# Input transfers first, the first weight conversion spread over the filter's units, and the fourth pair's last steps moved into the second MLP step

## The chip, the cores and the metric

The kernel runs on one core of one Trainium2 chip. TensorE (PE) multiplies; VectorE (DVE), ScalarE (ACT) and GpSimd (POOL) do the elementwise work; SyncE (SP) issues transfers between HBM and SBUF, which 16 DMA engines carry. The metric is the device time of one execution in microseconds (us); the time before is 1118.43 us, the median of three runs (1118.03 to 1119.11).

## The reference

Three stages follow one another on 6016 tokens of 256 channels. The first is a circular convolution along the sequence, written with Fourier transforms; the other two are MLPs with 2048 hidden units.

```python
X = np.fft.rfft(x, axis=1)                     # x: 2 x 3008 x 256
F = (filt_r + 1j * filt_i)[None, :, :]
x = np.fft.irfft(X * F, n=3008, axis=1).reshape(6016, 256)
h = x @ w_in;  x = np.maximum(0.01 * h, h) @ w_out        # first MLP
h = x @ w_in2; r = np.maximum(h, 0); out = (r * r) @ w_out2   # second MLP
```

The weights come as 64-bit floats and are used as 32-bit floats.

## The kernel before

**The filter.** The length 3008 is split as 47 x 64. The 256 channels are cut into 16 groups of 16, so with two batches there are 32 *units*; unit s is batch s mod 2 of group s // 2. The loop over s (lines 704 to 751) is a software pipeline: iteration s holds the first transform of unit s (`stage_a`, matmul `pa`), its transpose on VectorE (`stage_r`, tile `bin`), the second transform of unit s-1 (`stage_b`, matmul `px`), the product with the filter (`stage_s`: ScalarE copies px to `xc`, VectorE makes `t1` from px and `fr`; `stage_2`: GpSimd makes `t2` from xc and `fi`), the inverse transform of unit s-3 (`stage_i`, matmuls into `zps`) and its transpose (`stage_t`, tile `zin`). `fi` must first get its signs: the first groups by `sign_f` on VectorE or GpSimd, the later ones by `sign_k` on ScalarE, one column a time. Units in `SWAP` need one `zps` matmul instead of two, but an addition before it (`stage_y`, on VectorE for `SWAP_V`, else on GpSimd).

**The last transform** (`stage_o`, matmuls `pi`, and `stage_w`, a copy to SBUF) runs for the first 128 channels inside the loop's second half, and for the other 128 after it (`fill`), 16 groups of 4 matmuls each; four PSUM tiles take turns, so a group needs the copy of the group four before it. `OUT_V` names the groups whose copy VectorE makes; ScalarE makes the rest.

**The MLPs.** Weights are taken in eight *pairs* of 128 hidden columns for each layer. One *step* is one pair on one block of 2 x 512 (or 2 x 480) tokens. Within a step `up` makes the hidden values with seven block products instead of eight (three matmuls each, a high and a low part of every factor), VectorE adds partial products from PSUM (`plus`: v, u and three h), ScalarE and GpSimd apply the activation and split it (`g`, `gp`), and `down` multiplies by w_out.

**Conversion of weights.** `narrow_w` turns one pair from 64 to 32 bits in two halves, k = 0 (w_in) and k = 1 (w_out): `size` on ScalarE; `clamp`, `upper`, `signed`, `exp`, `low` on VectorE; `add`, `sums` on GpSimd mostly; then `hi` on ScalarE and `lo` split the result into two parts. `load` fetches the next pair's words (tile `wraw`, 512 KB) once `low` has read the old ones.

**What sets the order.** Each engine runs its instructions in the order in which the code issues them. The conversion is put between the other work by two clocks: F ticks four times in an iteration of the unit loop and once in a `fill`, M ticks eight times in an MLP step. The tables `NARROW_F` (four pairs, F clock) and `NARROW_1`, `NARROW_2` (M clock, from a start) say at which tick each part is issued. SP issues transfers in program order too, and a transfer waits until the one eight places before it in the program has completed, since eight completion semaphores take turns. Before the first unit, `WARM` matmuls of zeros keep TensorE going, and `MORE_WARM` more stand in iterations 1 to 3.

## Time and profile before

| | us |
|---|---|
| median of three runs | 1118.43 |
| the profiled execution, whole | 1117.95 |
| its span | 1116.2 |
| TensorE busy | 1104.2 (99%) |
| GpSimd busy | 760.6 (68%) |
| ScalarE busy | 666.0 (60%) |
| VectorE busy | 636.8 (57%) |

The profiled execution took 1.75 us beyond its span. A share of busy time is a mean over stages: in the filter, the first 119 us, VectorE and ScalarE are busy far more than in the MLPs. The waits of an engine tell where it stood still and for whom; the DMA share is that of the 16 engines.

### The profile page before, as it was taken

How to read it: one execution, taken by the hardware profiler on the slowest of the kernel's cores; microseconds unless marked ns; L12 is line 12 of the kernel's file. 1: busy time of each engine (PE TensorE's matmuls, PEld its weight loads, DVE VectorE, ACT ScalarE, POOL GpSimd, SP SyncE). 2: the span in 40 equal slices, each digit the busy share in tenths (PEclk: the TensorE clock that was granted, in tenths of full speed). 3: DMA queues.
4: the chain of work that ended last, by engine and by line, in shares of the span. 5: the costliest groups of instructions: out<-in, count | busy, mean ns of one | idle time of the engine just before them, and what ended most of it. 6: DMA issues, size and time to landing. Idle time of an engine off the chain costs nothing.

```text
span 1116.2 us, 14327 instructions
## 1 busy us (share of the span) xinstructions
PE 1104.2 (99%) x4824; PEld 885.4 (79%) x4824; DVE 636.8 (57%) x863; ACT 666.0 (60%) x1239; POOL 760.6 (68%) x617
## 2 busy tenths in 40 slices
PE   8999899999999999999999999999999999999998
PEld 5567778888888888888888888888888888888887
DVE  7999878857746746846745644434434335334332
ACT  3875565556545655655656766556556556556554
POOL 5777797777767758758769777547547547547544
PEclk9999999999999999999999999999999999999999
DMA  8644802144221121121122220200200200200100
GB/s 254 203 138 132 291 22 77 57 151 149 83 83 64 55 83 65 58 80 64 38 83 86 88 90 1 74 0 1 76 1 1 73 1 1 74 1 1 38 1 36
DMA packets 35386, 80.16 MB, mean 72 GB/s; under 512 B 4560, under 2 KB 14896, under 8 KB 35312
## 3 DMA queue, kind: packets, MB, share of 16 engines
q1 hardware_dynamic: 35312, 79.25, 21.2%
q8 instruction: 38, 0.62, 0.2%
q14 instruction: 36, 0.29, 0.1%
HBM read 51.31 MB, written 27.92 MB: 71 GB/s over the span
## 4 chain that ended last, share of the span: by engine, by line
PE 91%; DVE 2%; DMA 2%; POOL 1%; issue 1%; ACT 1%; SPq 1%; DVEq 0%; POOLq 0%; ACTq 0%
PE py L487 46%; PE ph L386 40%; PE pa L595 1%; PE zps L637 1%; PE pi L653 1%; PE px L607 1%; DMA fi<-in_fi 1%; DMA xop_b<-xop 1%; POOL gp L409 0%; DMA xin<-in_x 0%; DVE t L632 0%; PE zps L639 0%; DVE zin L646 0%; SPq L566 0%; ACT fi L591 0%
## 5 line engine op out<-in xcount | busy, mean ns | idle before, releaser
L409 POOL TENSOR_TENSOR gp<-g,gp 128x512 fp32r<-128x512 f32 (+1 forms) x384 | 506.8, 1325 | 312.3 <-ACT gp L408 101.0
L487 PE MATMUL py<-gp,wao 128*128 128x512 f32 (+1 forms) x1152 | 287.2, 390 | 0.2 <-POOL gp L409 0.2
L487 PE MATMUL py<-gp,wbo 128*128 128x512 f32 (+1 forms) x1152 | 286.6, 391 | 0.0
L386 PE MATMUL ph<-xop,wai 128*128 128x512 f32 (+1 forms) x1008 | 254.1, 391 | 2.5 <-DVE h L420 2.5
L487 PEld LDWEIGHTS py<-gp,wao 128*128 128x128 f32 x1152 | 215.9, 187 | 48.3 <-POOL gp L409 0.7
L386 PE MATMUL ph<-xop,wbi 128*128 128x512 f32 (+1 forms) x1008 | 253.9, 390 | 0.0
L487 PEld LDWEIGHTS py<-gp,wbo 128*128 128x128 f32 x1152 | 216.0, 188 | 47.8 <-POOL gp L409 0.3
L386 PEld LDWEIGHTS ph<-xop,wai 128*128 128x128 f32 x1008 | 188.9, 188 | 44.5 <-DVE h L420 3.1
L386 PEld LDWEIGHTS ph<-xop,wbi 128*128 128x128 f32 x1008 | 189.0, 187 | 41.7
L420 DVE TENSOR_TENSOR u<-ph,v 128x512 f32<-128x512 f32 (+1 forms) x96 | 65.3, 680 | 174.2 <-PE ph L386 174.2
L399 ACT ACTIVATE g<-h 128x512 f32<-128x512 f32 (+1 forms) x144 | 89.4, 621 | 106.3 <-DVE h L420 105.1
L407 ACT ACTIVATE g<-h 128x512 f32<-128x512 f32 (+1 forms) x144 | 89.2, 619 | 89.3 <-DVE h L416 88.6
L420 DVE TENSOR_TENSOR v<-ph,p 128x512 f32<-128x512 f32 (+1 forms) x96 | 64.9, 676 | 121.2 <-PE ph L386 117.5
L416 DVE CUSTOM_DVE_ANT_0 h<-ph,u 128x512 f32<-128x512 f32 (+1 forms) x96 | 65.2, 679 | 84.0 <-PE ph L386 82.2
L420 DVE TENSOR_TENSOR h<-ph,u 128x512 f32<-128x512 f32 (+1 forms) x96 | 65.2, 679 | 55.3 <-PE ph L386 53.7
L440 ACT ACTIVATE p<-ph 128x512 f32<-128x512 f32 (+1 forms) x96 | 56.3, 587 | 54.6 <-PE ph L386 54.6
L400 ACT ACTIVATE gp<-h 128x512 fp32r<-128x512 f32 (+1 forms) x144 | 87.7, 609 | 0.0
L408 ACT ACTIVATE gp<-h 128x512 fp32r<-128x512 f32 (+1 forms) x144 | 87.6, 609 | 0.0
L405 ACT ACTIVATE r<-ph 128x512 f32<-128x512 f32 (+1 forms) x48 | 28.2, 587 | 67.6 <-PE ph L386 67.5
L399 ACT ACTIVATE g<-ph 128x512 f32<-128x512 f32 (+1 forms) x48 | 28.2, 587 | 59.9 <-PE ph L386 56.6
L362 DVE TENSOR_TENSOR xop<-x,xop 128x512 fp32r<-128x512 f32 (+1 forms) x33 | 49.2, 1489 | 14.8 <-ACT xop L356 9.8
L625 POOL TENSOR_TENSOR t<-xc,fi 128x384 f32<-128x384 f32 x32 | 33.5, 1047 | 15.1 <-ACT xc L615 8.6
(199 smaller groups left out, 1061.2 us busy)
## 6 DMA issues: line engine op xcount, KB each, us to landing
wraw<-in_w SPq DMA_DIRECT2D x32, 512.0 KB
xin<-in_x SPq DMA_DIRECT2D x32, 160.0 KB
xt<-xo SPq DMA_DIRECT2D x26, 188.0 KB
yt<-o SPq DMA_DIRECT2D x16, 256.0 KB
x<-yt SPq DMA_DIRECT2D x4, 1024.0 KB
out<-o SPq DMA_DIRECT2D x16, 256.0 KB
w<-wi SPq DMA_DIRECT2D x8, 448.0 KB
wi<-w SPq DMA_DIRECT2D x8, 448.0 KB
```

Source lines behind the costliest of these rows:

```text
L362: eng.tensor_tensor(t[:, 1, :n], x_f32[v][name], t[:, 0, :n].bitcast(F32), ALU.subtract)
L386: nc.tensor.matmul(ph[:, :n], w[:, i, k], x[:, j, :n], start=(first and a == 0), stop=(a == 2), skip_group_check=True)
L399: nc.scalar.activation(g[:, :n], h[:, :n], AF.Prelu, alpha=0.01)
L400: nc.scalar.activation(t[:, 0, :n], h[:, :n], AF.Prelu, alpha=0.01)
L407: nc.scalar.activation(g[:, :n], h[:, :n], AF.Square)
L408: nc.scalar.activation(t[:, 0, :n], h[:, :n], AF.Square)
L409: nc.gpsimd.tensor_tensor(t[:, 1, :n], g[:, :n], t[:, 0, :n].bitcast(F32), ALU.subtract)
L416: nc.vector._custom_dve(dve_ops.TENSOR_ADD_SAT, out=t[:, :n], in0=ph[:, :n], in1=s[:, :n], s0=F32_MAX, s1=0.0)
L420: nc.vector.tensor_tensor(t[:, :n], ph[:, :n], s[:, :n], ALU.add)
L440: nc.scalar.activation(p1[:, :n], ph[0][:, :n], AF.Copy)
L487: nc.tensor.matmul(acc[c, t][:, :n], w[:, j, 2 * f + c], g[:, k, :n], start=(p == p0 and f == t and a == 0), stop=(p == p1 - 1 and f != t ...
L625: nc.gpsimd.tensor_tensor(t2, xc, fi_of(units[s][1], units[s][1] + 1), ALU.mult)
```

## The change

Five things change. The first input `xin` is issued right after the matrix `ra`; the five other constant matrices go from SP to ScalarE's queue; the first pair's first words (`wraw`) follow the fourth input instead of leading, and its second words are issued in iteration 3 by a new step `more`. The warm-up has 14 matmuls instead of 30. The first pair's conversion starts at F tick 7 instead of 0 and takes until tick 53, and the signs of the first four `fi` groups are made one iteration later. Unit 3's addition goes from VectorE to GpSimd, and the copies of groups 9 and 12 go from VectorE to ScalarE. The fourth pair's second half ends seven F ticks later, and the first pair of the M clock has a table of its own, `NARROW_4`, with later ticks; the starts of the next three move by 2 to 4 ticks.

```diff
-WARM = 30
+WARM = 14
-SWAP_V = (3, 16, 17, 18, 20, 21, 25, 26, 27, 29, 30)
+SWAP_V = (16, 17, 18, 20, 21, 25, 26, 27, 29, 30)
-OUT_V = (0, 2, 9, 12)
+OUT_V = (0, 2)
-STARTS_1 = (0, 32, 48, 64)
+STARTS_1 = (0, 36, 52, 66)
 NARROW_F = (
-        size0=0, clamp0=0, upper0=0, signed0=2, exp0=4, low0=5, add0=8, sums=13, hi_i=20, lo_i=21, size1=20, clamp1=23,
...
+        size0=7, clamp0=11, upper0=11, more=14, signed0=15, exp0=19, low0=23, add0=26, size1=28, sums=29, clamp1=31,
...
-        upper1=150, sums=151, signed1=152, exp1=154, hi_i=155, lo_i=156, low1=160, load1=161, add1=162, hi_o=163,
-        lo_o=164,
+        upper1=150, sums=151, signed1=152, exp1=154, hi_i=155, lo_i=156, low1=167, load1=168, add1=169, hi_o=170,
+        lo_o=171,
...
+NARROW_4 = dict(
+    size0=4, clamp0=13, upper0=15, signed0=17, exp0=19, low0=21, load0=22, size1=24, add0=27, sums=30, clamp1=33,
+    upper1=35, signed1=36, hi_i=36, lo_i=37, exp1=37, low1=39, load1=40, add1=43, hi_o=44, lo_o=45,
 )
...
+        steps = {"more": lambda: load_w(layer, p, 1), "sums": sums, "out_i": lambda: put(0), "out_o": lambda: put(1)}
...
         nc.sync.dma_start(ra, c_ra)
+        for t, c in ((cb, c_cb), (sg, c_sg), (ci, c_ci), (cs, c_cs), (dd, c_dd)):
+            nc.scalar.dma_start(t, c)
...
-        load_w(0, 0, 0)
         load_x(0)
         load_x(1)
-        nc.sync.dma_start(cb, c_cb)
-        nc.sync.dma_start(sg, c_sg)
         load_fr(0)
         load_fi(0, 1)
         load_x(2)
-        nc.sync.dma_start(ci, c_ci)
-        nc.sync.dma_start(cs, c_cs)
         load_x(3)
+        load_w(0, 0, 0)
         load_fr(1)
         load_fi(1, 2)
         load_x(4)
-        load_w(0, 0, 1)
-        nc.sync.dma_start(dd, c_dd)
...
-            if s % 2 == 0 and s // 2 < SIGN[0][0]:
+            if s % 2 and s // 2 < SIGN[0][0]:
                 sign_f(s // 2)
...
-            begin("M", narrow_w(0, p, "N1"), NARROW_1, STARTS_1[p - NWA])
+            begin("M", narrow_w(0, p, "N1"), NARROW_4 if p == NWA else NARROW_1, STARTS_1[p - NWA])
```

The first place is ScalarE at the start. `wm` is the result of `size` for the first pair, `xc` the copy for units 0, 1, 2; before:

```order
L225 ACT_TABLE_LOAD
L225 ACTIVATE wm_197<-wraw0_165 128x512
L617 ACTIVATE xc_219<-px_212 128x384
L617 ACTIVATE xc_237<-px_230 128x384
L617 ACTIVATE xc_262<-px_252 128x384
```

and with the change:

```order
L553 DMA cb_113<-in_cb 128x128
L553 DMA sg_116<-in_sg 128x24
L553 DMA ci_114<-in_ci 128x128
L553 DMA cs_115<-in_cs 128x128
L553 DMA dd_117<-in_dd 128x128
L623 ACT_TABLE_LOAD
L623 ACTIVATE xc_191<-px_187 128x384
L229 ACTIVATE wm_196<-wraw0_169 128x512
L623 ACTIVATE xc_211<-px_205 128x384
L623 ACTIVATE xc_236<-px_228 128x384
```

Five transfers now stand ahead of the table load, and `size` stands between the copies of units 0 and 1 instead of ahead of both.

The second place is VectorE in the first four units, after its memsets: `bin` are the transposes of units 0 to 3, `t1` the products of units 0 to 2, `fi0` the signs, and `wm`, `wb_`, `wi32` the first pair's conversion; before:

```order
L228 TENSOR_SCALAR wm_197<-wm_197 128x512
L232 TENSOR_SCALAR wb__200<-wm_197 128x512
L602 STREAM_TRANSPOSE bin_202<-pa_195 128x512
L235 SCALAR_TENSOR_TENSOR wb__200<-wraw0_165,wb__200 128x512
L240 TENSOR_SCALAR wi32_214<-wb__200 128x512
L246 SCALAR_TENSOR_TENSOR wm_197<-wraw0_165,wi32_214 128x512
L602 STREAM_TRANSPOSE bin_217<-pa_210 128x512
L619 TENSOR_TENSOR t1_221<-px_212,fr_175 128x384
L602 STREAM_TRANSPOSE bin_235<-pa_228 128x512
L619 TENSOR_TENSOR t1_239<-px_230,fr_175 128x384
L587 TENSOR_TENSOR fi0_161<-fi0_161,sg_116 128x384
L602 STREAM_TRANSPOSE bin_260<-pa_250 128x512
```

and with the change:

```order
L608 STREAM_TRANSPOSE bin_179<-pa_177 128x512
L608 STREAM_TRANSPOSE bin_189<-pa_185 128x512
L625 TENSOR_TENSOR t1_193<-px_187,fr_160 128x384
L608 STREAM_TRANSPOSE bin_209<-pa_203 128x512
L625 TENSOR_TENSOR t1_213<-px_205,fr_160 128x384
L232 TENSOR_SCALAR wm_196<-wm_196 128x512
L236 TENSOR_SCALAR wb__219<-wm_196 128x512
L608 STREAM_TRANSPOSE bin_232<-pa_226 128x512
L625 TENSOR_TENSOR t1_238<-px_228,fr_171 128x384
L593 TENSOR_TENSOR fi0_150<-fi0_150,sg_116 128x384
L239 SCALAR_TENSOR_TENSOR wb__219<-wraw0_169,wb__219 128x512
L652 STREAM_TRANSPOSE zin00_118<-zps0_121 128x16x16x2
```

The five conversion steps have left the place ahead of unit 1's transpose; two now stand behind `t1` of unit 1, the third behind the signs, the others further on.

The third place is VectorE in the first MLP step, where v, u and h belong to the partial products `ph1` to `ph3`, and `wo32`, `wao` to the fourth pair's second half; before:

```order
L420 TENSOR_TENSOR v_1326<-ph1_1315,p1_1321 128x512
L246 SCALAR_TENSOR_TENSOR wm_1126<-wraw1_1077,wo32_1273 128x512
L420 TENSOR_TENSOR u_1349<-ph3_1317,v_1326 128x512
L420 TENSOR_TENSOR h_1351<-ph2_1316,u_1349 128x512
L254 TENSOR_TENSOR wo32_1273<-wb__1226,wm_1126 128x512
L291 TENSOR_TENSOR wao_1363<-wo32_1273,wao_1363 128x512
L420 TENSOR_TENSOR h_1371<-ph1_1315,u_1349 128x512
L420 TENSOR_TENSOR h_1391<-ph2_1316,v_1326 128x512
```

and with the change:

```order
L424 TENSOR_TENSOR v_1310<-ph1_1299,p1_1305 128x512
L424 TENSOR_TENSOR u_1328<-ph3_1301,v_1310 128x512
L424 TENSOR_TENSOR h_1330<-ph2_1300,u_1328 128x512
L424 TENSOR_TENSOR h_1348<-ph1_1299,u_1328 128x512
L424 TENSOR_TENSOR h_1368<-ph2_1300,v_1310 128x512
L250 SCALAR_TENSOR_TENSOR wm_1110<-wraw1_1061,wo32_1257 128x512
L424 TENSOR_TENSOR v_1390<-ph1_1374,p1_1380 128x512
L258 TENSOR_TENSOR wo32_1257<-wb__1210,wm_1110 128x512
```

The five additions of the first step now stand together, and the three conversion steps follow among those of the second step.

## Rows read from the trace of the kernel before

**Rows 1.** The page, busy time of each engine.
```profile
PE 1104.2 (99%) x4824; PEld 885.4 (79%) x4824; DVE 636.8 (57%) x863; ACT 666.0 (60%) x1239; POOL 760.6 (68%) x617
```
**Rows 2.** Waits of TensorE, whole span: us in total, times, longest.
```profile
PE px L607 <- DVE bin L602: 2.8, 4, 1.1
PE ph L386 <- DVE h L420: 2.5, 2, 2.0
...
PE pi L653 <- DVE xo L670: 0.9, 1, 0.9
...
PE py L487 <- POOL gp L409: 0.2, 1, 0.2
```
**Rows 3.** Stretches: length, busy time of each engine, PEclk, DMA share, GB/s.
```profile
0.00:5.00 5.00, 3.82 (x18) 3.82 (x19) 1.73 (x4) 1.28 (x1) 0.20 (x4) 1.00 0.55 144
5.00:10.00 5.00, 5.00 (x26) 3.25 (x24) 3.24 (x5) 1.17 (x2) 1.47 (x1) 1.00 0.85 247
...
30.00:50.00 20.00, 20.00 (x58) 10.60 (x57) 18.77 (x31) 16.61 (x42) 15.22 (x15) 1.00 0.63 189
...
150.00:1112.50 962.50, 962.26 (x4205) 788.03 (x4203) 506.33 (x671) 569.94 (x1032) 651.39 (x514) 1.00 0.15 53
```
**Rows 4.** Warm-up in two stretches (ns min/median/max, starts); `pa` of units 0, 3.
```profile
L551 PE MATMUL warm<-warm x15: 415/415/579, 1.2 to 4.3; 128*128 128x256 f32 x15
...
L551 PE MATMUL warm<-warm x15: 278/282/395, 4.5 to 6.3; 128*128 128x256 f32 x15
...
6.45 1.09 PE L595 MATMUL pa<-xin,ra 94*128 94x512 f32 x2
...
12.41 1.02 PE L595 MATMUL pa<-xin,ra 94*128 94x512 f32 x2
```
**Rows 5.** Start: first input in the chain, and ScalarE's wait for weight words.
```profile
1.66 4.41 DMA xin<-in_x
...
5.46 0.68 ACT L225 ACTIVATE wm<-wraw 128x512 f32<-128x512 f32 x1 [3.44 <-DMA wraw<-in_w]
```
**Rows 6.** Waits of VectorE from 7 to 45 us: total, times, longest.
```profile
DVE t L619 <- ACT xc L615: 2.2, 3, 1.0
DVE fi L587 <- DMA fi<-in_fi: 1.2, 1, 1.2
DVE bin L602 <- PE pa L595: 0.5, 1, 0.5
DVE t L619 <- ACT xc L617: 0.5, 1, 0.5
```
**Rows 7.** VectorE's conversion steps and unit 3's addition: duration ns min/median/max, starts.
```profile
L228 DVE TENSOR_SCALAR wm<-wm x7: 411/670/1114, 6.2 to 102.5; 128x512 f32<-128x512 f32 x7
...
L235 DVE SCALAR_TENSOR_TENSOR wb__200<-wraw,wb__200 x1: 649/649/649, 8.2 to 8.2; 128x512 int32<-128x512 int32 x1
...
L240 DVE TENSOR_SCALAR wi<-wb__200 x1: 1116/1116/1116, 8.9 to 8.9; 128x512 int32<-128x512 int32 x1
...
L246 DVE SCALAR_TENSOR_TENSOR wm<-wraw,wi x3: 692/825/1110, 10.1 to 82.5; 128x512 f32<-128x512 uint32 x3
...
L632 DVE TENSOR_TENSOR t<-t,t x1: 1349/1349/1349, 22.7 to 22.7; 128x384 f32<-128x384 f32 x1
```
**Rows 8.** Group 9's copy on VectorE, and ScalarE's two waits near it.
```profile
113.92 0.63 ACT L356 ACTIVATE xop<-x 128x512 fp32r<-128x512 f32 x1 [1.10 <-DVE x L351]
...
116.35 0.54 DVE L670 COPY xo<-pi 128x376 f32<-128x376 f32 x1
...
116.46 0.63 ACT L356 ACTIVATE xop<-xs 128x512 fp32r<-128x512 f32 x1 [1.91 <-DVE xs L351]
```
**Rows 9.** VectorE in the first MLP step: `low`, the first h, `lo`.
```profile
121.21 2.14 DVE L246 SCALAR_TENSOR_TENSOR wm<-wraw,wo 128x512 f32<-128x512 uint32 x1
...
123.98 0.69 DVE L420 TENSOR_TENSOR h<-ph,u 128x512 f32<-128x512 f32 x1
...
126.41 1.34 DVE L291 TENSOR_TENSOR wao<-wo,wao 128x512 fp32r<-128x512 f32 x1 [1.14 <-ACT wao L287]
```

More of the change, by code (lines that the diff above doesn't have):

```diff
@@ L73 @@
     dict(
-        size0=0, clamp0=0, upper0=0, signed0=2, exp0=4, low0=5, add0=8, sums=13, hi_i=20, lo_i=21, size1=20, clamp1=23,
-        upper1=27, load0=28, signed1=31, exp1=35, low1=39, add1=42, load1=44, hi_o=46, lo_o=49,
+        size0=7, clamp0=11, upper0=11, more=14, signed0=15, exp0=19, low0=23, add0=26, size1=28, sums=29, clamp1=31,
+        upper1=31, load0=32, signed1=35, hi_i=36, exp1=39, lo_i=40, low1=43, load1=44, add1=46, hi_o=50, lo_o=53,
     ),
     dict(
-        size0=40, clamp0=43, upper0=47, signed0=51, exp0=59, low0=63, add0=66, load0=68, size1=68, sums=70, clamp1=71,
+        size0=40, clamp0=47, upper0=47, signed0=51, exp0=59, low0=63, add0=66, load0=68, size1=68, sums=70, clamp1=71,
         hi_i=74, upper1=75, lo_i=77, signed1=79, exp1=83, low1=87, add1=90, load1=92, hi_o=93, lo_o=97,
@@ L94 @@
     upper1=15, signed1=15, exp1=15, hi_i=16, lo_i=16, low1=16, load1=16, add1=19, hi_o=20, lo_o=21,
+)
+NARROW_4 = dict(
+    size0=4, clamp0=13, upper0=15, signed0=17, exp0=19, low0=21, load0=22, size1=24, add0=27, sums=30, clamp1=33,
+    upper1=35, signed1=36, hi_i=36, lo_i=37, exp1=37, low1=39, load1=40, add1=43, hi_o=44, lo_o=45,
 )
@@ L265, in put @@
             nc.sync.dma_start(w2_d[p][:, 7 * k : 7 + 4 * k], w[k])
-        steps = {"sums": sums, "out_i": lambda: put(0), "out_o": lambda: put(1)}
+        steps = {"more": lambda: load_w(layer, p, 1), "sums": sums, "out_i": lambda: put(0), "out_o": lambda: put(1)}
         for k in range(2):
```

## The prediction

> **What bounds the kernel now.** I read the busy times first, then TensorE's waits, then the stretches, and last the instructions around each wait. TensorE is busy 1104.2 of 1116.2 us [rows 1]: a change can win only where TensorE waits, or before its first useful matmul. From 150 us on it has 962.26 busy of 962.50 us [rows 3], so nothing after 150 us has anything to give, and what is won earlier moves the end by as much. The waits are few [rows 2]: 2.8 us for the transposes `bin`, 0.9 for a copy `xo`, 2.5 for two h of the MLP, 0.2 for gp. Ahead of all of them, the first real matmul starts at 6.45 us, right behind the thirty warm-up matmuls, which end there [rows 4]; its input landed at 1.66 + 4.41 = 6.07 us [rows 5].
>
> The waits for `bin` are VectorE's lateness. VectorE is busy 18.77 of 20 us between 30 and 50 us [rows 3], while TensorE is not held up there: in the filter the two are nearly level, so an earlier first matmul is worth only what VectorE can follow.
>
> **The start.** The warm-up's first fifteen matmuls start between 1.2 and 4.3 us, 0.22 us apart, and take 415 ns; the next fifteen start 0.13 us apart and take 282 ns [rows 4]. So the engine nearly doubles its rate at about 4.7 us (from its lower level, 1.2 GHz, to 2.4), though the view's granted-clock column reads 1.00 throughout [rows 3]. Fourteen matmuls at the lower rate end at 1.18 + 14 x 0.215 = 4.2 us. The input now takes the second place in the queue, where the weight words landed by 5.46 us [rows 5]. It has 188 KB for their 512; the 344 KB (0.35 MB) less, at 144 to 247 GB/s [rows 3], make it 1.4 to 2.4 us sooner, and the 64 KB of `cb` on the other queue 0.3 to 0.5 later again: 3.4 to 4.6 us, which has the end of the warm-up inside. I take 4.2 for the first matmul, 2.25 us earlier, and give 0.3 back because half of its work lies before 4.7 us and runs at the lower rate. VectorE's first transpose then comes 1.95 us earlier.
>
> **What VectorE does with it.** From its first transpose to that of unit 13 I count what changes in its queue.
> - Waits that stand in it today: 2.2 + 1.2 + 0.5 + 0.5 = 4.4 us [rows 6]. The 1.2 goes, because the signs move an iteration later and that transfer leads the second words; so does the 0.5 for the first transpose.
> - Waits that come. ScalarE's `size` now stands between two copies xc, and `t1` of unit 1 stands behind its copy. `size` needs the first words, and ahead of them and with them are four inputs, fr, fi, ra and the constants, 1.96 MB (four times 188, 512, two times 192, 48 and 268 KB). At 144 GB/s for 5 us and then 247 [rows 3] that is 5 + (2.01 - 0.72) / 0.247 = 10.2 us. Then 0.68 for `size` [rows 5], which has 512 columns, and 0.5 for the copy, which has 384: `t1` of unit 1 starts at 11.4 us. From `pa` of unit 0 to that of unit 3 it is 12.41 - 6.45 = 5.96 us today [rows 4], 4.9 without the longest wait of 1.1 [rows 2], so VectorE would be ready at about 4.2 + 4.9 = 9.1 and waits 2.3 us, after some 0.9 in short waits for the first units. New waits 3.2 us; of the 2.7 for copies in today's list I keep 0.7, as VectorE runs closer behind.
> - Work. `clamp` and `upper`, 0.42 each when short, come into the stretch, 0.85 us; they lay before the first transpose. Unit 3's addition leaves, 1.35 [rows 7]; GpSimd, busy 15.22 of 20 us even later on [rows 3], has room for it. The five steps also meet GpSimd now, which worked only 1.47 of the 5 us from 5 to 10 [rows 3], where they ran before. `clamp` over the filter has 0.41, 0.67 and 1.11 us as shortest, median and longest, `low` 0.69, 0.83 and 1.11, while `exp` had 1.12 already [rows 7]. I add 0.4 us.
>
> In sum 1.95 + 4.4 - 3.2 - 0.7 - 0.85 + 1.35 - 0.4 = 2.55 us. Some waits of TensorE for `bin` further on stay, so I take 2.4. From below: each of the five at its longest (1.1 instead of 0.42, 0.42, 0.65, 1.12 and 0.69: 2.2 us more, of which 0.4 is counted) and the first words 0.6 later leave 0; from above, no contention, no kept wait and the words 0.6 sooner give 4.1.
>
> The same `clamp` takes from 411 to 1114 ns, the short one at 6.2 us, where GpSimd stood idle [rows 7, 3]. The Trainium skill, "SBUF — State Buffer", section "Who interferes with whom", says that VectorE, in certain modes or with two operands in SBUF, and GpSimd share one pair of ports under an exclusive lock held for a whole instruction; the trace agrees by those durations. By that rule every moved step that meets GpSimd pays for one of its instructions, and the sum would be at its lower bound; by the rows' medians it is 2.4.
>
> The moved constants cost ScalarE five issues ahead of its table load. No row has an issue on ScalarE; SP has its third transfer out at 1.66 us [rows 5], so 0.6 us each at most there. Five of them and the table load, ScalarE's 1.28 us in the first stretch [rows 3], end by 4.3 us, or 5 if ScalarE starts late. The first copy can't come before unit 1's matmul is done, about 6.5: no cost, and 1 us only if an issue took over a microsecond. SP's order has a wait instead: by the eight-place rule the second input's two parts wait for ra and cb to land, 2.5 to 4 us by the same rates, and it is needed at about 5.5, behind unit 0's matmul of 1.09 us, partly at the lower rate. I take nothing.
>
> **The copies.** TensorE's 0.9 us wait is for group 9's copy, which VectorE starts at 116.35 [rows 2, 8]. On ScalarE it follows the `xop` of 113.92, done at 114.55, so group 13 no longer waits. But group 10's copy stands behind the next `xop`, which waits for VectorE until 116.46 and ends at 117.1; with 0.5 for the copy, group 14 stalls about half a microsecond. I take 0.4 of 0.9; bounds 0 and 1.1, the latter if VectorE, rid of 0.54 us, is ahead.
>
> **The first MLP step.** Before, the 2.14 us `low`, the 0.68 `add` and the 1.34 `lo` with its 1.14 wait for ScalarE [rows 9] stand between v, u and the h; TensorE waits 2.5 us, one of the two waits 2.0 [rows 2]. With the change the five additions stand together. The first h, which cost 0.5 of the 2.5, started at 123.98 behind u, and u behind `low`; both can move up as far as u's product allows. The second h, which cost 2.0, stood behind `add`, `lo` and its wait, 3.2 us between 124.6 and 127.7 that go. I take the whole 2.5; the lower bound is 1.5, if u's product comes so late that h still misses TensorE. Next in line are the moved steps themselves, in step two, beside five additions of 0.69, and `add`, of the same shape: 6 x 0.69 + 2.14 + 1.34 = 7.6 us. A step takes TensorE 962.5 / 94 = 10.2 us (rows 3; 94 of the 96 steps lie there), which covers them.
>
> **The later pairs.** `NARROW_4` moves GpSimd's part of the fifth pair away from the `xs` sums, which took the 0.2 us wait for gp [rows 2]: 0.2 us, between -0.5 (the same meeting at a later tick) and 0.5.
>
> Sum: 2.4 + 0.4 + 2.5 + 0.2 = 5.5 us. The profiled execution took 1117.95 us (1116.2 and 1.75 around it), which becomes 1112.45. It lies 0.48 under the median of the runs, so the forecast for that is 1112.9.
>
> **Rivals.**
> - *VectorE eats the start.* For it: 18.77 of 20 us busy, and five steps moved under GpSimd. Against: 4.4 us of its own waits. The filter gives 0 to 0.5, the total is 3.3, 1115.1 us. Chance 0.17.
> - *VectorE isn't the limit.* The words land sooner, GpSimd is seldom met, the 1.95 and 2.15 of the 2.8 us for `bin` come through: 4.1, in total 7.2, 1111.2 us. Chance 0.15.
> - *The stall moves one step on.* `low`, `add` and `lo` stand between v, u and h in step two as they did in step one. For it: `low` took 2.14 there. Against: TensorE has other products then, `down` of step one. It gives 2.0 of the 2.5 back: 3.5, 1114.9 us. Chance 0.08.
> - *Slower: the clock.* The warm-up ends before the rise at 4.7 us. If the gaps of the first units (waiting for inputs, transposes) keep TensorE at the lower rate, its work up to unit 3, 4.9 us, takes twice that; each further unit costs 2 us or more (5.96 / 3, rows 4). The first 4.9 and one unit more eat all 5.5, so it decides from unit 4: with units 3 to 5 slow it is 4.9 + 6 - 5.5 = 5.4 us over, 1123.8. Against: today's wait of 1.1 us among the first units [rows 2] is followed by a `pa` no longer than the first, 1.02 against 1.09 us [rows 4]. Chance 0.04. The Trainium skill, "TensorE: Matmul & The Clock Gate", section "Part 1: The HAM clock gate (the "warmup" mystery)", has the clock released by sustained activity and throttled by default; by that rule a shorter warm-up is the thing to distrust, and the rows agree as far as the first rise.
>
> **From this to the numbers.** The forecast has 0.56 (its own range 1111.6 to 1114.4). The range for all, 1110.6 to 1115.8 us, holds the first three rivals at their centres. Within 0.2%, 2.2 us of 1118.43, this kernel can't be told from no change: that takes a gain under 2.2, the lower ends of the first and third rivals together, 0.08; slower by more 0.04; faster 0.88.
>
> **What would show it.** Right: the first `pa` at 4.1 to 4.4 us; `size` of the first pair ending near 10.9 with ScalarE waiting over 1 us for the words; no wait of TensorE for h in the first step; the second step still 10.5 us. VectorE without a pause from 11 to 45 us. Wrong: matmuls of the first units at twice today's duration; a TensorE wait over 1 us for `bin` beyond unit 8; a wait for h in step two; waits for `wm` behind 150 us from the shifted starts.

## The result: slower, 1125.6 us against 1118.7

The changed kernel takes 1125.59 us (median of 4, 1123.58 to 1127.50), the kernel before 1118.72 on the same chip (4 runs): a ratio of 1.0060, 95% interval 1.0047 to 1.0073. The forecast was 1112.9, so the sign is wrong. The profiled execution took 1127.5 us with a span of 1125.6. In part of the executions of most kernels the granted clock is lower for some 3 us and the time is 1.7 us longer (the kernel before, in one set of thirty: 1118.26 us for fifteen of them, 1120.00 for the others), so the traces below are compared stage by stage.

The busy times [answering to rows 1] hardly move, for the work is the same; only sixteen warm-up matmuls are gone:

```profile
PE 1107.1 (98%) x4808; PEld 884.7 (79%) x4808; DVE 638.1 (57%) x860; ACT 665.1 (59%) x1241; POOL 760.9 (68%) x618
```

To see where the time goes, I count matmuls from the last one back and compare the start of the same matmul in both traces (us; plus is later than in the kernel before):

| start in the kernel before | 15.2 | 49.5 | 108.1 | 120.8 | 143.9 | 165.4 | 186.4 | 207.4 | 228.4 | 249.4 | 1092 |
|---|---|---|---|---|---|---|---|---|---|---|---|
| changed kernel | +0.2 | +4.8 | +4.8 | +4.4 | +1.8 | +1.3 | +2.5 | +3.6 | +7.1 | +7.4 | +7.4 |

So the filter's start loses 4.8 us, the copies win 0.4, the first MLP steps win 3.1, and 165 to 249 us loses 6.1. The last 2.0 of the 9.4 us between the two spans lie behind the last matmul: the last output took 5.0 us to land instead of 3.0, which no other kept trace shows.

TensorE's waits over the whole span [rows 2] (total, times, longest) show the same: the waits for `h` are longer, and a wait for the input `xin` is new.

```profile
PE ph L390 <- DVE h L424: 4.0, 4, 2.4
PE pa L601 <- DMA xin<-in_x: 3.0, 2, 2.1
PE px L613 <- DVE bin L608: 2.9, 4, 1.6
...
PE pi L659 <- ACT xo L666: 0.6, 1, 0.6
PE py L491 <- ACT o L517: 0.5, 1, 0.5
```

Stretches of the changed kernel (columns as in rows 3: length, busy time of PE, PEld, DVE, ACT, POOL with counts, granted clock, DMA share, GB/s), and behind them two of the kernel before that rows 3 did not have:

```profile
10.00:30.00 20.00, 16.88 (x43) 8.39 (x43) 12.66 (x22) 7.13 (x18) 8.85 (x11) 0.91 0.82 237
30.00:50.00 20.00, 17.40 (x48) 8.51 (x47) 19.33 (x28) 16.66 (x41) 18.00 (x18) 1.00 0.71 216
...
130.00:165.00 35.00, 35.00 (x152) 28.16 (x151) 23.77 (x30) 23.04 (x43) 28.76 (x22) 1.00 0.37 134
165.00:249.00 84.00, 79.50 (x336) 62.24 (x335) 66.39 (x83) 46.77 (x83) 65.36 (x54) 1.00 0.22 76
```
```profile
10.00:30.00 20.00, 17.34 (x49) 8.61 (x49) 17.18 (x28) 10.15 (x25) 13.20 (x14) 1.00 0.96 295
...
165.00:249.00 84.00, 84.00 (x362) 67.58 (x361) 60.45 (x79) 48.44 (x86) 64.85 (x52) 1.00 0.27 95
```

Read the VectorE column (third): from 10 to 30 us it is busy 12.66 us where it was 17.18, and from 30 to 50 us it is full, 19.33 against 18.77 [rows 3], while TensorE now does 17.40 instead of 20.00. Work has left a stretch with room and come into one without. From 165 to 249 us the conversions fall on a TensorE that had no idle time before and has 4.5 us of it now. (A wait is listed from the modelled end of the matmul before it; by the starts of the matmuls around them the five waits in that stretch cost 5.7 of the 6.1 us.)

**The start, closer.** The first real matmul starts at 4.34 us, but unit 4's input lands at 15.4, and unit 4 starts 0.2 us later than in the kernel before. TensorE's rows there:

```profile
12.53 0.81 PE L645 MATMUL zps<-t,cs 128*128 128x384 f32 x2
15.42 1.10 PE L601 MATMUL pa<-xin,ra 94*128 94x512 f32 x2 [2.08 <-DMA xin<-in_x]
16.60 1.32 PE L613 MATMUL px<-bin,cb 128*128 128x384 f32 x2
17.71 1.49 PE L643 MATMUL zps<-t,ci 128*128 128x384 f32 x2
...
20.27 1.08 PE L601 MATMUL pa<-xin,ra 94*128 94x512 f32 x2
```

Behind the 2.08 us wait the same pairs of matmuls take 1.49 us instead of 0.81: the granted clock is at its lower level, 1.2 of 2.4 GHz, for some 3 us (0.50 from 17 to 20 us), and unit 4 takes 4.85 us where the start alone (below) at full clock took 2.87. ScalarE, meanwhile, stands with `size` between two copies until the words land at 13.06 us (10.2 was reckoned), and VectorE's `t1` of unit 1 behind it:

```profile
13.06 0.66 ACT L229 ACTIVATE wm<-wraw 128x512 f32<-128x512 f32 x1 [4.23 <-DMA wraw<-in_w]
```
```profile
14.14 0.56 DVE L625 TENSOR_TENSOR t<-px,fr 128x384 f32<-128x384 f32 x1 [3.72 <-ACT xc L623]
```

Where the time is lost for good is units 9 to 15. VectorE's conversion steps between `pa` of unit 9 (32.07 us) and of unit 15 (50.55), changed kernel; they sum to 7.52 us:

```profile
32.27 1.10 DVE L236 TENSOR_SCALAR wb__351<-wm 128x512 int32<-128x512 int32 x1
...
34.97 0.67 DVE L239 SCALAR_TENSOR_TENSOR wb__351<-wraw,wb__351 128x512 int32<-128x512 int32 x1
...
37.23 1.60 DVE L244 TENSOR_SCALAR wo<-wb__351 128x512 int32<-128x512 int32 x1
...
40.43 0.77 DVE L250 SCALAR_TENSOR_TENSOR wm<-wraw,wo 128x512 f32<-128x512 uint32 x1
...
42.80 0.78 DVE L232 TENSOR_SCALAR wm<-wm 128x512 f32<-128x512 f32 x1
43.62 1.11 DVE L236 TENSOR_SCALAR wb__463<-wm 128x512 int32<-128x512 int32 x1
...
46.32 1.49 DVE L239 SCALAR_TENSOR_TENSOR wb__463<-wraw,wb__463 128x512 int32<-128x512 int32 x1
```

and between the same units (30.93 to 45.79 us) in the kernel before, 4.27 us:

```profile
31.39 0.85 DVE L240 TENSOR_SCALAR wo<-wb__346 128x512 int32<-128x512 int32 x1
...
33.83 0.67 DVE L246 SCALAR_TENSOR_TENSOR wm<-wraw,wo 128x512 f32<-128x512 uint32 x1
...
36.98 1.11 DVE L228 TENSOR_SCALAR wm<-wm 128x512 f32<-128x512 f32 x1
...
39.69 0.51 DVE L232 TENSOR_SCALAR wb__481<-wm 128x512 int32<-128x512 int32 x1
...
41.93 1.13 DVE L235 SCALAR_TENSOR_TENSOR wb__481<-wraw,wb__481 128x512 int32<-128x512 int32 x1
```

Two steps more, and the shared ones longer: 3.25 us, of the 3.62 that these six units take longer (18.48 against 14.86).

**From 165 us on, closer.** Pairs are numbered here as p in the code, from 0: pair 4 is the fifth, the first on the M clock, which has `NARROW_4`; pairs 5 to 7 are the three with shifted starts; the moved operations are the fourth pair's, p = 3. VectorE between the first and the second `h` of a step, changed kernel:

```profile
211.30 0.69 DVE L424 TENSOR_TENSOR h<-ph,u 128x512 f32<-128x512 f32 x1
211.91 0.42 DVE L232 TENSOR_SCALAR wm<-wm 128x512 f32<-128x512 f32 x1
212.36 0.57 DVE L236 TENSOR_SCALAR wb__2142<-wm 128x512 int32<-128x512 int32 x1
212.97 1.68 DVE L239 SCALAR_TENSOR_TENSOR wb__2142<-wraw,wb__2142 128x512 int32<-128x512 int32 x1
214.68 1.40 DVE L244 TENSOR_SCALAR wo<-wb__2142 128x512 int32<-128x512 int32 x1
216.11 2.46 DVE L250 SCALAR_TENSOR_TENSOR wm<-wraw,wo 128x512 f32<-128x512 uint32 x1
218.50 0.68 DVE L424 TENSOR_TENSOR h<-ph,u 128x512 f32<-128x512 f32 x1
```

and in the kernel before:

```profile
207.65 0.69 DVE L420 TENSOR_TENSOR h<-ph,u 128x512 f32<-128x512 f32 x1
208.26 1.81 DVE L254 TENSOR_TENSOR wo<-wb__2100,wm 128x512 f32<-128x512 f32 x1
210.77 1.00 DVE L291 TENSOR_TENSOR wbo<-wo,wbo 128x512 fp32r<-128x512 f32 x1 [0.70 <-ACT wbo L287]
211.69 0.68 DVE L420 TENSOR_TENSOR h<-ph,u 128x512 f32<-128x512 f32 x1
```

From `h` to `h` it is 4.04 us before, with TensorE never waiting, and 7.20 now. A step has eight ticks, and on VectorE they stand as v, ticks 0 and 1, tick 2, u, h, ticks 3 to 5, h, tick 6, h, tick 7. `NARROW_1` has `clamp1`, `upper1`, `signed1`, `exp1` at 15 and `low1` at 16. With a start of 32 these are ticks 7 and 0 of a step, behind its last `h`. With 36 or 52 they are ticks 3 and 4, between two `h`. With 66 they are 1 and 2, ahead of u.

### The profile page after: what moved, and what is told of

Read it like the earlier page. It is cut to its first block, busy times and chain, and to the rows that moved or that the text cites. A ratio compares the mean times of both kernels' runs of the same rounds, so it can differ in the third digit from the quotient of the medians.

```text
span 1125.6 us, 14300 instructions
## 1 busy us (share of the span) xinstructions
PE 1107.1 (98%) x4808; PEld 884.7 (79%) x4808; DVE 638.1 (57%) x860; ACT 665.1 (59%) x1241; POOL 760.9 (68%) x618
## 4 chain that ended last, share of the span: by engine, by line
PE 90%; DVE 4%; ACT 2%; DMA 2%; issue 1%; POOL 1%; SPq 0%; ACTq 0%; DVEq 0%; POOLq 0%
PE py L491 45%; PE ph L390 40%; PE pi L659 2%; PE px L613 1%; PE zps L643 1%; PE pa L601 1%; ACT fi L597 1%; DMA wraw<-in_w 1%; DMA xin<-in_x 1%; DVE h L424 0%; ACT xc L621 0%; POOL t L631 0%; DVE wo L244 0%; DVE bin L608 0%; POOL t L638 0%
## 5 line engine op out<-in xcount | busy, mean ns | idle before, releaser
L424 DVE TENSOR_TENSOR h<-ph,u 128x512 f32<-128x512 f32 (+1 forms) x96 | 65.0, 678 | 49.2 <-PE ph L390 47.6
```

The source lines that it names most:

```text
L424: nc.vector.tensor_tensor(t[:, :n], ph[:, :n], s[:, :n], ALU.add)
```

## The experiments

Each kernel ran in a set with the kernel before on the same chip. Medians in us, number of runs, and the ratio with its 95% interval:

| run | time | before in its set | ratio |
|---|---|---|---|
| starts_back | 1123.13 (5) | 1119.66 (15) | 1.0035 (1.0023 to 1.0048) |
| late_back | 1123.16 (5) | 1119.66 | 1.0033 (1.0021 to 1.0046) |
| moved_alone | 1118.53 (11) | 1119.66 | 0.9995 (0.9986 to 1.0004) |
| start_alone | 1123.33 (5) | 1119.66 | 1.0038 (1.0024 to 1.0052) |
| second_half_early | 1122.91 (5) | 1118.47 (16) | 1.0042 (1.0029 to 1.0055) |
| starts_alone | 1126.83 (5) | 1118.47 | 1.0068 (1.0055 to 1.0081) |
| add_later | 1118.23 (11) | 1118.47 | 0.9995 (0.9986 to 1.0004) |
| gap_filled | 1121.79 (6) | 1118.47 | 1.0028 (1.0016 to 1.0040) |
| words_first | 1123.42 (5) | 1118.82 (19) | 1.0041 (1.0028 to 1.0054) |
| table_back | 1120.31 (11) | 1118.82 | 1.0009 (1.0000 to 1.0018) |
| gp_too | 1115.98 (9) | 1118.82 | 0.9976 (0.9966 to 0.9986) |
| long_warm | 1121.95 (5) | 1118.82 | 1.0035 (1.0022 to 1.0048) |
| table_only | 1121.60 (7) | 1119.35 (30) | 1.0023 (1.0013 to 1.0033) |
| consts_only | 1120.65 (11) | 1119.35 | 1.0013 (1.0004 to 1.0022) |
| pair4_only | 1119.23 (11) | 1119.35 | 0.9999 (0.9991 to 1.0008) |
| x4_first | 1121.17 (11) | 1119.35 | 1.0020 (1.0012 to 1.0029) |
| all_together | 1118.23 (11) | 1119.80 (15) | 0.9993 (0.9984 to 1.0002) |

TensorE against the kernel before, as in the first table:

| | 49.5 | 108.1 | 120.8 | 143.9 | 165.4 | 186.4 | 207.4 | 228.4 | 249.4 |
|---|---|---|---|---|---|---|---|---|---|
| starts_back | +4.1 | +4.2 | +3.9 | +1.3 | +0.8 | +4.1 | +4.7 | +4.7 | +4.7 |
| late_back | +5.3 | +5.4 | +5.1 | +3.4 | +4.9 | +4.9 | +4.9 | +4.9 | +4.9 |
| moved_alone | +0.8 | +0.8 | +0.5 | -1.3 | +0.5 | +0.5 | +0.5 | +0.5 | +0.5 |
| start_alone | +3.1 | +3.2 | +3.2 | +3.2 | +3.3 | +3.3 | +3.3 | +3.3 | +3.3 |
| starts_alone | +0.5 | +0.5 | +0.5 | +0.5 | +0.5 | +0.5 | +4.7 | +8.9 | +8.9 |
| add_later | +0.3 | +0.3 | 0.0 | -1.0 | +0.2 | +0.2 | +0.2 | +0.2 | +0.2 |
| gp_too | +0.2 | +0.2 | -0.2 | -1.9 | -2.2 | -2.2 | -2.2 | -2.2 | -2.2 |
| pair4_only | +0.5 | +0.5 | +0.5 | +0.5 | 0.0 | 0.0 | 0.0 | 0.0 | 0.0 |

**The late part: starts and table of the later pairs.**

```diff
 # starts_back: the changed kernel with
-STARTS_1 = (0, 36, 52, 66)
+STARTS_1 = (0, 32, 48, 64)
 # late_back: the same, and pair 4 on NARROW_1 again
-NARROW_4 if p == NWA else NARROW_1
+NARROW_1
 # starts_alone: the kernel before with
-STARTS_1 = (0, 32, 48, 64)
+STARTS_1 = (0, 36, 52, 66)
```

> The changed kernel with STARTS_1 as before, (0, 32, 48, 64); NARROW_4 and all else of the change stay. Theory A, the shifted starts: with starts that are no multiples of 8 the conversion steps of pairs 5 to 7 fall between v, u and h of a step, and TensorE loses 6 us between 165 and 249 us. Then these go: TensorE's wait for h falls from 4.0 to under 1 us, and the time is 5 to 6 us below the changed kernel's, about 1120. Theory B, the longer table NARROW_4 of pair 4 is what costs: then at most 1 us comes back, 1124.5 or more.

> The changed kernel with NARROW_1 for pair 4 too and STARTS_1 as before; start, moved operations and copies stay as changed. Both theories: 6 us of the loss go, about 1119.5. Theory A: within 1 us of the run with the starts alone put back. Theory B: all 6 us come here and not there.

> The kernel before with STARTS_1 = (0, 36, 52, 66) as its only edit; pair 4 keeps NARROW_1. Theory A: starts that are not multiples of 8 put four or five conversion steps between the two h's of a step; TensorE loses 1.2 + 1.2 + 3.5 us as in the changed kernel between 170 and 230 us, in all 4 to 6 us: 1123 to 1125. Theory B': the loss needs the longer table as well, whose last steps run into pair 5: at most 1.5 us slower than before.

starts_alone is theory A without doubt: the starts alone lose 8.4 us, more than the 4 to 6 expected, and all of it between 186 and 228 us. Its rows there, 21 us each:

```profile
186.00:207.00 21.00, 18.62 (x74) 14.63 (x73) 17.33 (x21) 9.33 (x17) 13.27 (x12) 0.92 0.08 27
207.00:228.00 21.00, 18.61 (x74) 14.62 (x73) 16.01 (x21) 10.86 (x21) 14.84 (x13) 0.92 0.22 75
```

Each has one wait of 2.4 us for `h`, and a granted clock of 0.92 behind it; 2 x 2.4 is 4.8, and 0.08 of 21 us, twice, is 3.4: together 8.2 of the 8.4.

starts_back and late_back say that the starts are not all, and neither came at a time that was expected. The starts put back recover 6.07 - 3.95 = 2.1 us of what is lost behind 165 us, with `NARROW_4` staying (+0.8 to +4.7). The waits for `h` do go (4.0 to 0.4 us, as theory A has it), but a wait of 2.3 us for a copy `o` that VectorE makes takes their place: the table runs to tick 45 and pair 5 begins at 32, so two conversions share the fifth and sixth step. With both back nothing is lost behind 165 us, but the 3.1 us won between 121 and 165 us shrink to 0.2. The two edits belong together: the longer table keeps the first steps free, and its end at tick 45 is a reason to start the others later.

**The moved operations, alone and with the next stalls moved too.**

```diff
 # moved_alone: the kernel before with
-low1=160, load1=161, add1=162, hi_o=163, lo_o=164
+low1=167, load1=168, add1=169, hi_o=170, lo_o=171
-OUT_V = (0, 2, 9, 12)
+OUT_V = (0, 2)
 # add_later: and, for pair 4,
+NARROW_4 = dict(NARROW_1, add1=23, hi_o=24, lo_o=25)
 # gp_too: and
+NARROW_4 = dict(NARROW_1, add1=23, hi_o=24, lo_o=25, lo_i=34)
 # pair4_only: gp_too without the first four lines
```

> The kernel before with two edits of the change alone: low1, add1, hi_o, lo_o of the fourth pair seven ticks later, and OUT_V = (0, 2). Theory C, these terms stand by themselves: the waits for h in the first MLP step (2.5 us) and part of that for xo (0.3) go, 1118.7 - 2.9 = 1115.8 us. Rival: the gain seen in the changed kernel came only from a TensorE that arrived 4.5 us later, so that VectorE had caught up; then 0 to 1 us, 1118.

It won nothing. By 144 us TensorE is 2.1 us ahead of where it was at 108 (+0.8 to -1.3), and by 165 us 1.8 of that is gone. VectorE in the third step (counted from the first, that of rows 9; the expectation of add_later calls it the second):

```profile
144.06 0.69 DVE L420 TENSOR_TENSOR h<-ph,u 128x512 f32<-128x512 f32 x1
144.67 1.72 DVE L254 TENSOR_TENSOR wo<-wb__1505,wm 128x512 f32<-128x512 f32 x1
147.08 1.84 DVE L291 TENSOR_TENSOR wbo<-wo,wbo 128x512 fp32r<-128x512 f32 x1 [0.70 <-ACT wbo L287]
148.84 0.68 DVE L420 TENSOR_TENSOR h<-ph,u 128x512 f32<-128x512 f32 x1
```

These are pair 4's own operations, not the moved ones. They stood there before as well, and cost nothing because TensorE came some 2 us later.

> The kernel before with the moved operations and OUT_V = (0, 2), and pair 4's add1, hi_o, lo_o at ticks 23, 24, 25 instead of 19, 20, 21, behind the second step's last h instead of between its h's. Theory F: the run with the moves alone gained nothing because that addition (1.72 us) and lo (1.84 us with 0.70 of waiting) held the second step's h back by 1.8 us; then the 1.8 us stay won: 1116.5 us. Rival: the same two operations hold up step three, whose xop steps fill VectorE: 1118.3.

The wait of 1.2 us for `h` in the third step went, and TensorE met GpSimd there instead. A wait of 1.4 us for `h` in the second step, 0.6 in moved_alone, comes behind the moved operations, `low` (1.81 us here, 0.68 there) and `add`, with pair 4's `signed` (1.75 and 1.19) among them:

```profile
PE ph L387 <- DVE h L421: 1.4, 1, 1.4
...
PE py L488 <- POOL gp L410: 1.4, 1, 1.4
```

> The kernel before with the moved operations, OUT_V = (0, 2) and pair 4's add1, hi_o, lo_o at ticks 23 to 25, as run before, and pair 4's lo_i (GpSimd, 2.14 us) at tick 34 instead of 16, so that GpSimd no longer has it between two gp. Theory F': the 1.4 us that TensorE waited for gp in the third step goes, and nothing else comes: 1117.0. Rival: the four engines are all full between 140 and 165 us, and the 2.14 us hold up a later gp: 1118.2.

With `lo_i` off that place too the gain stays, 2.4 us from 108 us on, and the time is 1115.98 us: faster than both kernels. The medians differ by 2.8 us because none of its nine runs has the lower clock that 8 of the 19 of the kernel before have. The waits that are left in its MLPs, and the last copy:

```profile
PE ph L387 <- DVE h L421: 0.6, 1, 0.6
PE pi L654 <- ACT xo L661: 0.6, 1, 0.6
...
PE py L488 <- POOL gp L410: 0.2, 1, 0.2
```

> The kernel before with pair 4's add1, hi_o, lo_o at ticks 23 to 25 and lo_i at 34 as its only edit: fourth pair's last operations and copies as before. Theory K: two stalls lie one behind the other; taking the second away alone wins nothing, because in the kernel before TensorE comes to the second step late enough: 1118.3, while both edits together gave 1116.0. Rival: pair 4's steps are the whole gain: 1116.

Theory K: pair 4's steps alone are worth nothing (0.9999), the moved ones alone nothing (0.9995), both 2.4 us. Three stalls lay one behind the other, each hidden by the one ahead.

**The start.** `pa` of units 0, 4, 9 and 15, and from 9 to 15 (us):

| | unit 0 | 4 | 9 | 15 | 9 to 15 |
|---|---|---|---|---|---|
| before | 6.45 | 15.21 | 30.93 | 45.79 | 14.86 |
| changed | 4.34 | 15.42 | 32.07 | 50.55 | 18.48 |
| start_alone | 4.29 | 14.62 | 30.30 | 48.91 | 18.61 |
| second_half_early | 4.34 | 15.43 | 33.18 | 49.57 | 16.39 |
| gap_filled | 4.34 | 15.41 | 30.35 | 48.90 | 18.55 |
| long_warm | 6.33 | 14.49 | 32.25 | 49.22 | 16.97 |
| words_first | 7.40 | 17.89 | 31.34 | 49.86 | 18.52 |
| table_back | 7.53 | 16.70 | 32.01 | 47.29 | 15.28 |
| table_only | 6.46 | 14.18 | 32.50 | 49.48 | 16.98 |
| consts_only | 7.51 | 16.29 | 32.00 | 46.87 | 14.87 |
| x4_first | 4.34 | 13.28 | 29.50 | 47.25 | 17.75 |
| all_together | 4.34 | 13.11 | 30.95 | 47.78 | 16.83 |

```diff
 # start_alone: the changed kernel with STARTS_1, NARROW_4, OUT_V and the moved four as before
 # second_half_early: start_alone with
-size1=28, clamp1=31, upper1=31, signed1=35, exp1=39, low1=43, add1=46, hi_o=50, lo_o=53
+size1=24, clamp1=27, upper1=27, signed1=31, exp1=35, low1=39, add1=42, hi_o=46, lo_o=49
 # gap_filled: start_alone with
-MORE_WARM = (0, 2, 2, 2)
+MORE_WARM = (0, 2, 2, 2, 12, 0, 0, 8)
 # long_warm: start_alone with
-WARM = 14
+WARM = 30
 # words_first: start_alone with load_w(0, 0, 0) ahead of load_x(0)
 # table_back: words_first, NARROW_F[0] and [1] as before, load_w(0, 0, 1) behind load_x(4)
 # table_only: the kernel before with NARROW_F[0] and [1] as changed, second words by "more"
 # consts_only: the kernel before with the five constants on nc.scalar's queue
 # x4_first: start_alone with load_x(4) ahead of load_w(0, 0, 0)
 # all_together: x4_first + second_half_early's table + gp_too's edits
```

> The changed kernel's start alone (14 warm-up matmuls, inputs ahead of the words, constants on ScalarE's queue, first conversion over units 2 to 10, signs an iteration later, unit 3's addition on GpSimd), the rest as before. If the start by itself loses the 4.8 us that the aligned matmuls show by 50 us: 1118.7 + 4.8 = 1123.5. Rival: waits further on in the kernel before (0.9 for xo, 2.5 for h) swallow part of the delay, since VectorE has time to catch up: 1121 to 1122.

The start loses 3.1 us in this trace, at full clock throughout, and later waits swallow none of it.

> The changed kernel's start alone, but the second half of the first pair's conversion one unit earlier (size1 24, clamp1 and upper1 27, signed1 31, exp1 35, low1 39, as in the kernel before but for four ticks on the first two). Theory D: the start loses its 3.7 us between units 9 and 15 (30 to 49 us), because conversion steps left a stretch where VectorE waits for inputs and came into one where it is the bound, and last longer there. Then TensorE loses 1 to 3 us less between units 9 and 15 and the time is that much below the start alone. Rival E: what is lost follows from the late inputs of units 4 and 7: then the same time, within 0.5 us.

Units 9 to 15 take 2.2 us less, as theory D says, but unit 9 comes 2.9 later, so the time stays (1.0042 against 1.0038), which is the time of rival E: the steps went a unit back, to where ScalarE stands ahead of the signs' scaling until 25.1 us and VectorE behind ScalarE for 3.6 us. Neither theory had that cause.

> The changed kernel's start alone with one edit: the first weight words lead the transfers again, ahead of the inputs. Theory H: the start loses because the late words (13 us) hold ScalarE between two copies and VectorE behind it for 3.7 to 4.1 us, and because SP's next loads wait for their landing. Then VectorE's wait at 14 us goes, TensorE is at most 1.5 us behind the kernel before at 50 us instead of 3.1 to 3.8, and the time is about 1120. Theory D, that the later table by itself overfills VectorE between 30 and 50 us: the time stays within 0.7 us of the start alone (1122.5 to 1123.3).

Theory H falls. VectorE's wait for the words went, and unit 9 is 0.4 us behind the kernel before although unit 4 was 2.7 behind; then units 9 to 15 take 18.52 all the same. With the later table a delay ahead of unit 9 is hardly carried on: with unit 9 at 30.3 us unit 15 starts at 48.9 (start_alone, gap_filled), with unit 9 at 32.3 and 32.5 at 49.2 and 49.5 (long_warm, table_only). With the table of before it is carried on in full: in consts_only unit 9 and unit 15 are both 1.1 us late.

> As the run with the words first, and the first pair's and second pair's tables as in the kernel before too, with the second words loaded behind the fifth input. Left of the change are the 14 warm-up matmuls, the constants on ScalarE's queue, the signs an iteration later and unit 3's addition on GpSimd. If order and table are the whole loss of the start: within 0.7 us of the kernel before, 1118 to 1119. Rival: one of the parts left costs 1 us or more: 1119.5 or above.

With the table back, 9 to 15 take 15.28 and the time falls from 1123.4 to 1120.3. What stays, 1.0 us by the ratio (its interval begins at 1.0000) or 1.5 by the medians, is the rival's case: one of the parts left costs.

> The kernel before with the five constants issued on ScalarE's queue as its only edit. Theory J: their 268 KB travel beside the words and the first input instead of behind them, unit 0 starts 1 us later (7.5 us in the run with words and table put back, 6.45 before), and 1 to 1.5 us are lost: 1119.5 to 1120. Rival, the prediction's value: nothing, within 0.5 us.

It is the constants, as theory J has it: unit 0 starts at 7.51 us instead of 6.45, TensorE is 1.1 us behind at 49 us, and the ratio is 1.0013. The size is less sure than the sign: in the seven traces whose first transfers are those of the kernel before unit 0 starts anywhere from 6.45 to 7.25 us, and at 7.40 to 7.53 in the three with the constants on ScalarE's queue and the words first. The signs an iteration later and unit 3's addition on GpSimd were not run by themselves; table_back, which has them too, is no slower than this run.

> The kernel before with the changed tables of the first two pairs as its only edit (and the second words loaded at tick 14); transfers, warm-up, constants, signs as before. Theory D: the later table alone costs what TensorE lost between units 9 and 15 in all runs that have it, 2.1 to 3.7 us: 1120.5 to 1122. Rival E: it costs only with late inputs, since VectorE here has its waits among units 7 and 8 all the same: within 0.7 us of the kernel before.

The table alone costs 1.0023, and 2.1 us in units 9 to 15: theory D, at its lower end. TensorE's other 1.6 us lie ahead of unit 9, behind a 2.4 us wait for an input at 22.8 to 25.1 us, with a granted clock of 0.66 between 25 and 30 us.

> The changed kernel's start alone with 30 warm-up matmuls instead of 14, so that the first input's matmul starts at 6.4 us and not at 4.3. Theory I: unit 4's input, which lands at 14.6 to 15.4 us whatever the start, sets the pace, and the 2.1 us are worth nothing: the same time as the start alone within 0.5 us. Rival: the earlier start is worth its 2 us: 2 us slower. Second rival: the longer warm-up keeps the granted clock up later: 1 us faster.

Theory I: the first matmul two microseconds later or earlier makes no difference (1.0035 and 1.0038). Unit 4 starts at 14.5 with either.

> The changed kernel's start alone with the fifth input ahead of the first words. Theory L: unit 4 then comes at 12.5 to 13 us instead of 14.6 to 15.4, but unit 7 again at 24.6 (its input and the signs' filter piece land there), and the later table costs the same behind it: 1122 to 1123. Rival I: unit 4's late input is what took the two microseconds won at the start: 2 us faster, 1121.

The rival I has it: about 2 us faster than the start alone (1.0020 against 1.0038; the intervals just overlap, but both traces are at full clock and differ by 1.6 us). Unit 4 starts at 13.28; then TensorE waits 2.58 us for unit 3's `bin`, because VectorE stands behind the copy that stands behind the words.

> The changed kernel's start alone with 12 more warm-up matmuls ahead of unit 4 and 8 ahead of unit 7, where TensorE waits for inputs. Theory G: those waits of 1.4 to 2.4 us let the granted clock fall to its lower level later, which costs 2 us in most runs (spans 1119.4 at a mean clock of 1.000 and 1121.5 to 1122.6 at 0.997); with the gaps filled all runs show 1.000 and the median falls 2 us below the start alone. Rival: the clock falls as often, and the time is the same or 1 us longer.

Four of six runs show a mean clock of 1.000, against one of five without; the median is 1.5 us lower, but the intervals overlap (1.0016 to 1.0040, 1.0024 to 1.0052). The direction is as expected, its size is not settled.

> The changed start with the fifth input ahead of the first words and the second half of the first pair's conversion one unit earlier, STARTS_1 as before, the moved operations and OUT_V = (0, 2), and pair 4's add1, hi_o, lo_o at ticks 23 to 25, lo_i at 34. Theory M: late input and late table are the start's whole loss; without them it is no worse than the start before, and with the 2.5 us of the other edits the time is 1115 to 1117. Rival: the signs' filter piece, which holds ScalarE until 24 us, and VectorE behind it, keep the loss: 1118 to 1120.

The rival's time at its lower end, but not its place: 1118.23, level with the kernel before, and by the ratios 1.9 us above gp_too. The start is still 2.0 us behind at 49 us, so late input and late table are not its whole loss. The table above has these 2.0 us in units 9 to 15: unit 9 is level with the kernel before (30.95 against 30.93), although VectorE waits for the first words and the granted clock is 0.56 between 17 and 20 us in that trace. In units 9 to 15 VectorE has the same five conversion steps as the kernel before, 5.85 us of them instead of 4.27, and all of the difference is one `low`, 2.29 us where it took 0.67:

```profile
34.46 2.29 DVE L247 SCALAR_TENSOR_TENSOR wm<-wraw,wo 128x512 f32<-128x512 uint32 x1
```

GpSimd was busy 18.45 of the 20 us from 30 to 50 there, 15.22 in the kernel before [rows 3]; that the step is long because of it is not shown.

## Why the prediction was wrong, step by step

- **The start, "I take 2.4": it lost 4.8 (3.1 at full clock).** The failed step is "from its first transpose to that of unit 13 I count what changes in its queue". That sum treats VectorE as the limit all the way. It is not: up to unit 8 it waits for inputs, words and ScalarE (12.66 busy of 20 us from 10 to 30 us), and only from 30 us on it is full. With the later table a wait taken away ahead of unit 9 is worth next to nothing (words_first), and a step that comes behind it is paid (table_only, table_back). Instead of 0.85 us for `clamp` and `upper`, units 9 to 15 got 3.25 us more of conversion.
- **"2.25 us earlier" for the first matmul** came as said (4.34 us) and was worth nothing (long_warm), because unit 4's input has the same bytes ahead of it as before. I had priced VectorE's waits behind the start, and no input's landing behind the first.
- **The words, "10.2 us":** 13.06. The rates were about right (176, 236, 274 and 236 GB/s in the stretches from 1, 5, 10 and 12 us), which makes 2.7 MB by 13.06 us, where I had counted 2.01: transfers issued behind the words, at 7.0 to 9.7 us, travelled beside them.
- **The constants, "I take nothing":** 1.1 us in the trace of consts_only, where the words lead, and 1.0013 in its ratio. I had looked at ScalarE's issue time and not at the first input, which lands later; in the changed order that input is first, and it did not show.
- **The slower rival, the clock, 0.04:** one part of it came true in the profiled execution. Not from the shorter warm-up, though unit 0's pair took 1.98 us, the time of the lower level: the clock fell behind the 2.08 us wait and cost unit 4 two microseconds. The Trainium skill, "TensorE: Matmul & The Clock Gate", section "Part 1: The HAM clock gate (the "warmup" mystery)", has the clock throttled by default and released by sustained activity. The rows agree in that the granted clock falls to 0.50 behind a wait; that it does so in some executions only, they don't explain.
- **The copies, 0.4:** right, 0.3 to 0.4; the wait for `xo` is 0.6 instead of 0.9 [rows 2].
- **The first MLP step, 2.5:** in the trace it is there (no wait from 130 to 165 us, +4.4 to +1.3), but not as a gain of its own. The rival "the stall moves one step on", put at 0.08, is what happens to the moved operations by themselves: in step two TensorE waits 0.6 us (moved_alone) or 1.4 (add_later) behind them, and in step three 1.2 us behind pair 4's own addition and lo. "TensorE has other products then" was no argument: they are used up when it comes 2 us sooner. In the changed kernel step two has no such wait; its `NARROW_4` also takes pair 4's own steps out of that place.
- **The later pairs, 0.2 within ±0.5: lost 6.1.** The mis-sized term with the largest error. I followed GpSimd's part of pair 4 and looked at none of the VectorE steps of pairs 5 to 7, whose starts the same edit shifts from 0 to 4 or 2 modulo the step's eight ticks. The "would make it wrong" list named their waits for `wm`, which never came; it is the order on VectorE, not their data, that costs.

Summed by the trace: -4.8 + 0.4 + 3.1 - 6.1 = -7.4 us, where +5.5 was forecast.

## What to carry to other kernels

Before counting what an engine's queue gains and loses, split the stretch at the point from which that engine is full: here a wait taken away ahead of it was worth little (words_first, long_warm), though an earlier input was worth 1.6 us (x4_first), and conversion that came in behind it, 3.25 us, cost its whole length and more (3.62). When a table of due times repeats with a period, a shifted start is a change of place for every operation in it; read one period on each engine, and what stands between two results that the critical engine waits for. And a stall taken away is worth only the distance to the next one: here three had to go together (1116.0 us) before any of them showed.

## What the runs showed of the chip, and was not expected

- A wait of TensorE of 2.0 to 2.4 us can cost nearly as much again. In the run with the starts alone two waits of 2.4 us were each followed by a mean granted clock of 0.92 over 21 us, 1.7 us more; in the changed kernel one of 2.08 us cost 2.0 us more. The kernel before has one of 2.0 us at 126 us, for `h` in the first MLP step, and the changed kernel one of 2.4 us at 216, with 1.00 behind them. Behind the same wait for `h`, consts_only has the lower clock; its row first, then that of the kernel before:

```profile
130.00:135.00 5.00, 5.00 (x16) 3.94 (x16) 3.39 (x6) 2.62 (x7) 2.63 (x2) 0.66 1.03 417
```
```profile
130.00:135.00 5.00, 5.00 (x23) 4.04 (x22) 4.43 (x6) 2.95 (x6) 3.58 (x3) 1.00 1.02 405
```

add_later and gp_too, which lack that wait, have full clock (a mean of 0.999 or 1.000) in all 11 and all 9 of their runs; the kernel before has it in 11 of 16 and 11 of 19 in the same sets. So its longer executions probably come from this wait, but no trace of one was kept, and what decides it in a single execution these runs don't show.
- One operation of one shape on VectorE takes very different times by its neighbours: `low` (128x512) 0.67 us at 34 us in the kernel before and 2.46 at 216 in the changed one, `signed` 0.67 at 35 us and 1.68 at 213. Up to 240 us of both traces the steps that meet no GpSimd instruction all take their shortest times (`clamp` 0.41 to 0.43, `low` 0.66 to 0.69), and GpSimd is busy for two thirds or more of each step of over 1.2 us. The Trainium skill, "SBUF — State Buffer", section "Who interferes with whom", gives VectorE, in certain modes or with two operands in SBUF, and GpSimd one shared pair of ports under a lock held for a whole instruction. These durations agree with it, as does a GpSimd busy 18.00 of 20 us where the steps were long (30 to 50 us). No run here took GpSimd's work away to prove it.
- Transfers on a second queue are not free for the first: with 268 KB of constants moved to ScalarE's queue and the words leading, the first input's matmul starts at 7.40 to 7.53 us in three traces, at 6.45 to 7.25 in the seven without.
